# A planned gated-attention and mixture kernel: mixed inputs of the first block on TensorE, loads on a second queue, a wider search for the order

## The chip, the cores and the metric

The kernel runs on one core of one Trainium2 chip. The metric is device microseconds of one execution, and the median of three executions is given. A profile is of one execution more. Names in short: PE is TensorE (matrix products), DVE is VectorE, ACT is ScalarE, POOL is GpSimd, SP is the engine that issues transfers. PSUM is the memory that PE writes, in eight banks; SBUF is the memory on the chip that all engines read.

## What is computed

Three stages one after the other, each on the result of the one before: a gated linear attention over 8 heads of width 48, a mixture layer with a token shift, and a second mixture with a low-rank product over the tokens (4 batches, 768 tokens, 384 channels).

```python
for t in range(S):                                   # attention, for every head
    state = alpha[:, :, t, :, None] * state + einsum('bhd,bhe->bhde', k[:, :, t], v[:, :, t])
    y[:, :, t] = einsum('bhd,bhde->bhe', q[:, :, t], state)

x_prev = concatenate([zeros, x[:, :-1, :]], axis=1)  # first mixture
xk = mu_k * x + (1.0 - mu_k) * x_prev
xr = mu_r * x + (1.0 - mu_r) * x_prev
k = maximum(xk @ w_k, 0.0)
x = sigmoid(xr @ w_r) * (k * k @ w_v)

u = x + (x.transpose(0, 2, 1) @ U @ V).transpose(0, 2, 1)   # second mixture
out = u + maximum(u @ w_ch1, 0.0) @ w_ch2
```

The inputs are drawn so that alpha lies in 0.8 to 1.0. The attention of the fast path holds while alpha is at least 0.7072; the kernel checks this on its data and has a general path for the rest.

## The kernel before

**Tiling.** The 3072 tokens are 8 blocks of 384 (half a batch each). Attention works in units of two head pairs and 384 tokens (16 units, two to a block), a head pair being two heads in partitions 0 to 47 and 64 to 111 ("EV" and "OD"). A unit has two phases (`ph`), one for each head pair. For each phase `load_qka` brings q, k and alpha (one transfer for each head), `prep` makes decayed keys and queries with two scans on DVE (`L359`), `keys_by_token` transposes the keys on PE (`L320`), `scores` makes three 128x128 score tiles for each head on PE and masks them on DVE; for each unit `load_v` brings the values of the EV and of the OD heads in two transfers, `states` multiplies keys by values (`48x48`) and scans the sum, and `outputs` multiplies scores by values and states by queries and copies the result to x. Unit 1 stands before unit 0 in the first block (`first_attention`).

**Weights** come as 64-bit floats and are decoded on the chip in chunks of 128x384: two passes on ACT, two or three on DVE, of which the last (`split`) leaves a rounded high part and the rest as a low part. A product is three matrix products (`mm3`: high by high, high by low, low by high) in a rounded 32-bit type; nine of them of 384 columns make one tile of `moe1` or `moe2`.

**Mixed inputs** (`prep_mix`). In the first block each of the six tiles of xk and xr is `x_prev * (1 - mu)` on ACT, `x * mu + that` on DVE, and then a split on ACT and DVE.

**What sets the order.** Nothing is issued where it is written. Every operation is recorded with an engine, a cost in ns and a wished place (`plan.at`), and `Plan.issue` runs a list scheduler over the whole program: forward, then backward to get priorities, eleven times, and the order of the best forward pass is issued, so that each engine's queue is one fixed list. Where PE has nothing ready by the scheduler's costs, it puts in fillers, small bf16 products of a tile of zeros (`L405`), one for each 56 ns (112 ns in the first 4.5 us). These fillers are in PE's list for good: PE executes them whether or not there is anything to wait for.

**The end.** `check_range` reduces what the checks found, multiplies on PE (a 1x1 product) and casts the count on DVE into `ok_i` (`L1064`). `values_load` (`L407`) reads `ok_i` into a register of each engine, and `tc.If` (`L408`) branches past the general path. The mixed inputs' weights (`load_mu`) and all other transfers are issued from SP (`L376`).

```python
plan.act(t, x[:, kk, 0:TB], AF.Copy, scale=omm[:, j, kk : kk + 1])
plan.stt(t, x[:, kk, 1:], mu[:, j, kk : kk + 1], t, ALU.mult, ALU.add)
split(t, MIX[j][0][:, kk, :], MIX[j][1][:, kk, :], ...)
```

Of the kernel before, what the change touches and what calls it, by code (L numbers as in the profile page):

```python
# [8 lines left out]
F32 = mybir.dt.float32  # L9
# [10 lines left out]
P = 128  # L20
B, H, S, D = 4, 8, 768, 48
DM = 384
KD = 3
# [28 lines left out]
ROUNDS = 10  # L52
BATCH = 15000.0
# [27 lines left out]
class Plan:  # L81
# [7 lines left out]
    ENGINES = ("PE", "DVE", "ACT", "POOL", "SP")  # L89
    LAT = {"PE": 200.0, "DVE": 130.0, "ACT": 155.0, "POOL": 80.0, "SP": 1900.0}  # L90
    TO_PE = {"DVE": 250.0, "ACT": 270.0, "POOL": 200.0, "SP": 1900.0}
    OWN = {"PE": 0.0, "DVE": 127.0, "ACT": 150.0, "POOL": 100.0, "SP": 1900.0}
# [188 lines left out]
    def issue(self, filler=None, until=0.0, rounds=0):  # L281

        work = self.work
        n = len(work)
        after = [[] for _ in range(n)]
        before = [[] for _ in range(n)]
        for i, w in enumerate(work):
            for j in w[2]:  # L290
                lat = self.latency(j, i)
                after[j].append((i, lat))
                before[i].append((j, lat))
        n_after, n_before = [len(a) for a in after], [len(b) for b in before]
        prio = [w[4] for w in work]
        best = None
        for r in range(rounds + 1):
            order, times = self.schedule(after, n_before, prio, False, self.FILL, until)
            end = max(t for _, t in times)
            if best is None or end < best:  # L300
                best, self.order, self.times = end, order, times
            if r < rounds:
                _, back = self.schedule(before, n_after, [-t for _, t in times], True)
                prio = [-t if w[4] > self.AHEAD else w[4] for (_, t), w in zip(back, work)]
        for i in self.order:
            if i < 0:
                filler(-1 - i)
            else:
                self.run(*work[i][3])
# [12 lines left out]
    def act(self, out, in_, func, **kw):  # L322
# [3 lines left out]
        cost = (110.0 if in_.tensor.name in self.arenas else 68.0) + n * 0.833 + 95.0 * len(extra)  # L326
# [43 lines left out]
    def dma(self, out, in_, out_key=None, in_key=None, cost=650.0):  # L370
        words = 1
        for d in out.shape:
            words *= d
        self.add(
            "SP", max(cost, words / 56.0), [out if out_key is None else out_key], [in_ if in_key is None else in_key],
            lambda: self.nc.sync.dma_start(out, in_),  # L376
        )
# [3 lines left out]
def tile_gated_attention_moe(ctx, tc, qka, v, mus, w_k, w_r, w_v, U, V, w_1, w_2, out):  # L381
# [25 lines left out]
    n_ok = nc.values_load(ok_i[0:1, 0:1], min_val=0, max_val=2 * D, skip_runtime_bounds_check_because="a count of partitions")  # L407
# [4 lines left out]
def fast_path(nc, plan, arena, rounded, shared, banks, qka, v, mus, w_k, w_r, w_v, U, V, w_1, w_2, out, x2d, ok_i):  # L412
# [61 lines left out]
    Xs[1] = new(KD + 1, TB + 1)  # L474
    x2_ring = ring(2, DM)
# [187 lines left out]
    def load_mu():  # L663
        plan.dma(mu, mus, in_key="w")
        plan.dve(75, [omm], [mu], lambda: nc.vector.tensor_scalar(
            out=omm, in0=mu, scalar1=-1.0, scalar2=1.0, op0=ALU.mult, op1=ALU.add))

# [27 lines left out]
    def load_qka(ph, parts=((0, KD),), rows=D, to=None):  # L695
# [4 lines left out]
        for a, z in parts:  # L700
            for hh in range(2):
# [4 lines left out]
                    bass.AP(src.tensor, src.offset, [[KD * TB, n], [1, (z - a) * TB]]), in_key="in", cost=475.0,  # L706
# [134 lines left out]
    def first_attention():  # L841
# [3 lines left out]
        for i, u in enumerate((1, 0)):  # L845
# [5 lines left out]
            load_v(u)  # L851
            for j in range(2):
# [11 lines left out]
    def mm3(ps, lh, ll, rh, rl, first, last):  # L864
# [5 lines left out]
        plan.at = mm_at[0] - EARLY  # L870

# [196 lines left out]
    plan.at = -1640  # L1068
    load_mu()
# [21 lines left out]
    for n in range(NBLK):  # L1091
# [3 lines left out]
        if n:  # L1095
            prep_mix(n, (1, 0), start(n) - DUE["mix_r"], DUE["d1" if n == 1 else "d2" if n == 2 else "d"])
        else:
            prep_mix(n, (0,), start(n) - DUE["mix0_k"], "ACT")
            prep_mix(n, (1,), R0 - DUE["mix0_r"], "ACT")
# [309 lines left out]
```

## Time and profile before

| | |
|---|---|
| median of three executions | 699.4 us (698.97 to 699.49) |
| the profiled execution, its own time | 699.82 us |
| its span in the trace | 698.0 us |
| mean granted clock of PE | 0.998 of full speed |
| PE busy | 687.7 us (99%) |
| DVE, ACT, POOL busy | 479.9, 360.5, 66.8 us |
| moved by transfers | 55.14 MB |

The span reaches from the first to the last instruction that the profiler records; 1.8 us of the profiled execution's own time lie around it. PE's busy time counts the fillers too. A line such as `L138` or `L315` is that of a helper through which all operations of a kind go, so the rows are told apart by shapes and times. A matrix product of plain 32-bit floats is two records in the trace, one in the list of the order; a rounded one and a transpose are one record.

### The profile page before, as it was taken

The page shows a single profiled execution, that of the slowest core. Times are in us where ns is not written, and L with a number is a line of the kernel's source. Part 1 is how long each engine was busy: PE and PEld are TensorE (multiplying, and loading weights), DVE is VectorE, ACT ScalarE, POOL GpSimd, SP SyncE. Part 2 cuts the span into 40 slices and gives each one's busy share as a digit, 9 for nine tenths or more (in the row PEclk, how much of TensorE's full clock was granted, in tenths as well). Part 3 has the DMA queues.
Part 4 walks back from the last instruction along what each step waited for, and adds up shares of the span by engine and source line. Part 5 has one row for each costly group of instructions (what it writes and reads, how often), then busy time and mean ns, then how long its engine had stood idle before and what let it go on. Part 6 is the DMA issues. An engine that isn't in the chain of part 4 may idle for free.

```text
span 698.0 us, 13655 instructions
## 1 busy us (share of the span) xinstructions
PE 687.7 (99%) x5251; PEld 664.2 (95%) x5251; DVE 479.9 (69%) x1077; ACT 360.5 (52%) x895; POOL 66.8 (10%) x102
## 2 busy tenths in 40 slices
PE   9999999999999999999999999999999999999996
PEld 8899899999999999899999999999999999999996
DVE  7799898897567575663898976474858566574611
ACT  3779687868667586696997831111111212121210
POOL 2000104241211312101010100000000000000000
PEclk9999999999999999999999999999999999999999
DMA  8857674343231222313363502020100102020001
GB/s 193 209 140 193 145 168 132 93 133 76 78 80 50 85 70 77 78 40 99 96 193 91 147 1 69 0 69 2 58 12 11 58 1 69 0 69 1 36 1 38
DMA packets 29785, 55.14 MB, mean 79 GB/s; under 512 B 5360, under 2 KB 20816, under 8 KB 29712
## 3 DMA queue, kind: packets, MB, share of 16 engines
q1 hardware_dynamic: 29712, 54.19, 28.6%
q8 instruction: 43, 0.70, 0.4%
q14 instruction: 30, 0.25, 0.1%
HBM read 43.55 MB, written 9.44 MB: 76 GB/s over the span
## 4 chain that ended last, share of the span: by engine, by line
PE 85%; DVE 2%; ACT 1%; DMA 1%; issue 0%; SPq 0%; DVEq 0%; ACTq 0%
PE bank L315 84%; DMA arena<-in_qka_dram 1%; PE bank L320 1%; DVE shared L359 1%; ACT shared L330 1%; ACT arena L330 0%; DVE shared L138 0%; ACT bank L330 0%; DVE arena L138 0%; DVE rounded L138 0%; ACT rounded L330 0%; SPq L376 0%; DVE arena L730 0%; ACTq L330 0%; DVEq L138 0%
## 5 line engine op out<-in xcount | busy, mean ns | idle before, releaser
L315 PE MATMUL bank<-rounded 128*128 128x384 f32 x2232 | 421.1, 338 | 0.4 <-DVE rounded L138 0.4
L315 PEld LDWEIGHTS bank<-rounded 128*128 128x128 f32 x2232 | 383.1, 186 | 8.4 <-DVE rounded L138 1.2
L330 ACT ACTIVATE rounded<-bank 128x384 fp32r<-128x384 f32 x163 | 79.6, 489 | 188.8 <-PE bank L315 187.8
L315 PE MATMUL bank<-rounded,shared 128*128 128x384 f32 x864 | 164.5, 334 | 0.0
L315 PEld LDWEIGHTS bank<-rounded,shared 128*128 128x128 f32 x864 | 151.1, 188 | 0.0
L138 DVE SCALAR_TENSOR_TENSOR rounded<-bank,rounded 128x384 fp32r<-128x384 f32 x96 | 53.4, 556 | 105.1 <-ACT rounded L330 103.9
L330 ACT ACTIVATE arena<-arena 128x384 f32<-128x384 f32 (+5 forms) x234 | 102.2, 462 | 23.9 <-DMA arena<-in_qka_dram 16.7
L330 ACT ACTIVATE rounded<-arena 128x384 fp32r<-128x384 f32 (+3 forms) x134 | 68.6, 521 | 57.4 <-DVE arena L997 40.4
L997 DVE STREAM_TRANSPOSE arena<-arena 32x96 f32<-32x96 f32 x336 | 90.9, 271 | 5.0
L315 PEld LDWEIGHTS bank<-shared 128*48 128x48 f32 (+2 forms) x1408 | 75.7, 141 | 11.9 <-issue 6.9
L315 PE MATMUL bank<-shared 128*48 128x128 f32 (+3 forms) x1408 | 86.0, 264 | 0.2 <-DMA shared<-in_v_dram 0.2
L138 DVE SCALAR_TENSOR_TENSOR arena<-arena 128x384 int32<-128x384 int32 (+2 forms) x140 | 80.8, 592 | 7.9 <-ACT arena L330 7.2
L330 ACT ACTIVATE bank<-bank 128x384 f32<-128x384 f32 x128 | 61.0, 478 | 16.4 <-PE bank L315 15.1
L138 DVE TENSOR_TENSOR rounded<-bank,rounded 128x384 fp32r<-128x384 f32 x67 | 37.0, 552 | 39.5 <-ACT rounded L330 39.0
L359 DVE TENSOR_TENSOR_SCAN shared<-arena 112x384 f32<-112x384 f32 x64 | 60.8, 961 | 2.6 <-ACT arena L330 1.2
L138 DVE TENSOR_TENSOR rounded<-arena,rounded 128x384 fp32r<-128x384 f32 (+1 forms) x105 | 58.3, 564 | 4.4 <-ACT rounded L330 4.0
L138 DVE TENSOR_TENSOR arena<-bank,arena 128x384 f32<-128x384 f32 (+1 forms) x76 | 40.8, 550 | 20.2 <-PE bank L315 13.2
L330 ACT ACTIVATE arena<-bank 112x384 f32<-112x384 f32 (+3 forms) x62 | 28.7, 488 | 25.0 <-PE bank L315 24.5
L138 DVE TENSOR_TENSOR shared<-bank,arena 128x384 f32<-128x384 f32 x64 | 33.1, 547 | 9.4 <-PE bank L315 9.2
L138 POOL TENSOR_TENSOR rounded<-arena,rounded 128x384 fp32r<-128x384 f32 (+1 forms) x25 | 27.4, 1109 | 121.5 <-ACT rounded L330 107.4
L405 PE MATMUL bank<-warm 128*128 128x128 bf16 x584 | 37.4, 225 | 1.1 <-DVE arena L553 1.1
L405 PEld LDWEIGHTS <-warm 128*128 128x128 bf16 x584 | 35.2, 101 | 2.3 <-DVE arena L553 1.1
(48 smaller groups left out, 213.1 us busy)
## 6 DMA issues: line engine op xcount, KB each, us to landing
arena<-in_qka_dram SPq DMA_DIRECT2D x58, 216.0 KB, 3.9
arena<-in_w_dram SPq DMA_DIRECT2D x24, 384.0 KB, 3.5
shared<-in_v_dram SPq DMA_DIRECT2D x32, 144.0 KB, 2.4
x2d<-arena SPq DMA_DIRECT2D x24, 192.0 KB, 2.0
arena<-x2d SPq DMA_DIRECT2D x8, 576.0 KB, 4.1
out_dram<-arena SPq DMA_DIRECT2D x24, 192.0 KB, 1.9
arena<-in_w_v_dram SPq DMA_DIRECT2D x8, 384.0 KB, 3.8
arena<-in_w_k_dram SPq DMA_DIRECT2D x5, 384.0 KB, 7.6
```

The lines of the kernel that those rows point to most:

```text
L138: fn(**args)
L315: "PE", cost, [out], [lhsT, rhs], lambda out, lhsT, rhs: fn(out, lhsT=lhsT, rhs=rhs, start=start, stop=stop),
L320: self.add("PE", cost, [out], [in_, ident], lambda: self.nc.tensor.transpose(out, in_, ident))
L330: self.add("ACT", cost, outs, [in_] + extra, lambda out, in_: fn(out, in_, func, **kw), out=out, in_=in_)
L359: lambda: self.nc.vector.tensor_tensor_scan(out=out, data0=d0, data1=d1, initial=0.0, op0=op0, op1=op1), self.in_sbuf(d0, d1),
L405: lambda i: nc.tensor.matmul(banks[SPARE[i]][:, 384:512], lhsT=warm, rhs=warm, start=True, stop=True), FILL_UNTIL, ROUNDS
L997: plan.dve(284, [to], [src], lambda to=to, src=src: nc.vector.transpose(out=to, in_=src))
```

## The change

1. `n_ok = nc.values_load(...)` stands one level deeper, inside the scope of the tiles.
2. `Plan.issue` takes the best order of the eleven passes and makes 90 rounds more: the best order's priorities are shifted at random by up to 500 or 2000 ns, and three forward passes with two backward passes between them are tried. The best of all is issued.
3. A queue `ACTQ` is added: the OD loads of phases 2 and 3 (unit 1, the first to be needed) are issued from ACT. In the scheduler's costs ACTQ is a queue apart, that takes no time of ACT. A transfer's least cost is 580 ns where it was 650 (475 for q, k and alpha); a copy of a certain strided form on ACT costs more.
4. For the first block the mixed inputs are made on PE: `load_mu` is called early and makes 12 diagonal matrices (128x128) on ACT; `first_mix` multiplies each diagonal by x (two plain 32-bit products of 384 columns for each of six tiles, into banks 0, 1, 3 and 4), and the split reads the bank.

```diff
 ROUNDS = 10
+AROUND = 90
...
-        prio = [w[4] for w in work]
         best = None
-        for r in range(rounds + 1):
+
+        def there(prio):
+            nonlocal best
             order, times = self.schedule(after, n_before, prio, False, self.FILL, until)
             end = max(t for _, t in times)
-            if best is None or end < best:
-                best, self.order, self.times = end, order, times
...
+        prio = [w[4] for w in work]
+        for r in range(rounds + 1):
+            prio = back(there(prio))
+        rng = random.Random(1)
+        for r in range(AROUND):
+            far = (500.0, 2000.0)[r % 2]
+            prio = [p + rng.uniform(-far, far) if p > self.AHEAD else p for p in best[1]]
+            there(back(there(back(there(prio)))))
+        _, _, self.order, self.times = best
...
-        cost = (110.0 if in_.tensor.name in self.arenas else 68.0) + n * 0.833 + 95.0 * len(extra)
+        apart = in_.dtype == F32 and in_.ap[-1][0] == NC + 1
+        cost = (110.0 if in_.tensor.name in self.arenas else 68.0) + n * (2.2 if apart else 0.833) + 95.0 * len(extra)
...
-    n_ok = nc.values_load(ok_i[0:1, 0:1], min_val=0, max_val=2 * D, ...)
+        n_ok = nc.values_load(ok_i[0:1, 0:1], min_val=0, max_val=2 * D, ...)
...
         plan.dve(75, [omm], [mu], ...)
+        for j in range(2):
+            for kk in range(KD):
+                for a, t in enumerate((mu, omm)):
+                    plan.act(diag[:, a, j, kk], ident, AF.Copy, scale=t[:, j, kk : kk + 1])
...
-                    bass.AP(src.tensor, src.offset, [[KD * TB, n], [1, (z - a) * TB]]), in_key="in", cost=475.0,
+                    bass.AP(src.tensor, src.offset, [[KD * TB, n], [1, (z - a) * TB]]), in_key="in",
+                    queue="ACTQ" if hh and ph in (2, 3) and to is None else "SP",
...
+    def first_mix(j, due, into):
+        x = Xs[0]
+        for kk in range(KD):
+            plan.at = due + 3 * kk
+            ps = into[kk][:, 0:TB]
+            plan.mm(ps, diag[:, 0, j, kk], x[:, kk, 1:], True, False, 650.0)
+            plan.mm(ps, diag[:, 1, j, kk], x[:, kk, 0:TB], False, True, 650.0)
+            split(ps, MIX[j][0][:, kk, :], MIX[j][1][:, kk, :], "DVE")
...
-            prep_mix(n, (0,), start(n) - DUE["mix0_k"], "ACT")
-            prep_mix(n, (1,), R0 - DUE["mix0_r"], "ACT")
+            first_mix(0, start(n) - DUE["mix0_k"], (banks[0], banks[1], banks[3]))
+            first_mix(1, start(n) - DUE["mix0_k"] + 9, (banks[0], banks[1], banks[4]))
```

**Where the order moves.** On SP, after the first loads of phases 2 and 3, at the program's start, before the change (the names in brackets are the semaphores that a transfer waits for before it takes them itself; `in_v` rows are values, the first two those of unit 1):

```order
L376 DMA arena<-in_qka_dram 64x1152 [waits DMAHW0_49]
L376 DMA arena<-in_qka_dram 48x1152 [waits DMAHW1_49]
L376 DMA shared<-in_v_dram 128x288 [waits DMAHW2_49]
L376 DMA shared<-in_v_dram 128x288 [waits DMAHW3_49]
L376 DMA arena<-in_qka_dram 64x1152 [waits DMAHW4_49]
L376 DMA arena<-in_qka_dram 48x1152 [waits DMAHW5_49]
```

The same place after the change:

```order
L396 DMA shared<-in_v_dram 128x288 [waits DMAHW1_49]
L396 DMA arena<-in_qka_dram 48x1152 [waits DMAHW2_49]
L396 DMA arena<-in_qka_dram 64x1152 [waits DMAHW3_49]
L396 DMA arena<-in_qka_dram 48x1152 [waits DMAHW4_49]
L396 DMA arena<-in_qka_dram 64x1152 [waits DMAHW5_49]
L396 DMA shared<-in_v_dram 128x288 [waits DMAHW6_49]
```

And on PE after the change, the first products of keys by values (`48x48`, unit 1), with what they wait for (`bank_80<-shared 128x128` are the scores of phase 3's OD heads):

```order
L333 MATMUL bank_80<-shared 128x128 [waits DVE_49]
L333 MATMUL bank_80<-shared 128x128 x2
L425 LDWEIGHTS warm
L425 MATMUL bank_75<-warm 128x128
L333 MATMUL bank_78<-shared 48x48 [waits DMAHW6_49,Activation_49]
L333 MATMUL bank_78<-shared 48x48 [waits DMAHW1_49]
```

The two halves of unit 1's values stood together behind phase 0; now the four loads of phases 0 and 1 stand between them, and PE's first product waits for the later half. Ahead of that product PE's list holds 12 score products where it held 6, and 132 fillers where it held 126 (of both, 53 and 59 are the first run).

On PE, from the last outputs of the first attention on, after the change (`bank<-arena 128x384` are the products with a diagonal; `warm` are the fillers, of which one pair stands for each run of them):

```order
L333 MATMUL bank_80<-shared 48x128 x10
L333 MATMUL bank_76<-arena 128x384 x2
L333 MATMUL bank_77<-arena 128x384
L333 MATMUL bank_73<-arena 128x384 x2
L333 MATMUL bank_74<-arena 128x384 x2
L333 MATMUL bank_77<-arena 128x384
L333 MATMUL bank_76<-rounded 128x384
L425 LDWEIGHTS warm
L425 MATMUL bank_75<-warm 128x128
```

Before the change the fillers follow at once on the row `MATMUL bank_80<-shared 48x128 x10`. Counted over PE's whole list, there are 584 fillers before and 342 after. Up to the last product of the first attention they are 199 and 209 (the first run, in which PE starts, 59 and 53); from there to the first long run without fillers 385 and 108; and a run of 25 stands later, in the first block's products. The 12 products with a diagonal are the only real work added; 3168 products of 384 columns in the rounded type stand in both lists.

On DVE, at the program's end, before and after:

```order
L138 TENSOR_TENSOR arena<-bank_73,arena 128x384
L138 TENSOR_TENSOR arena<-bank_74,arena 128x384
L138 TENSOR_TENSOR arena<-bank_75,arena 128x384
L407 TENSOR_LOAD ok_i
L408 COMPARE_AND_BRANCH
```

```order
L140 TENSOR_TENSOR arena<-bank_73,arena 128x384
L140 TENSOR_TENSOR arena<-bank_75,arena 128x384
L140 TENSOR_TENSOR arena<-bank_74,arena 128x384
L1103 CAST ok_i<-bank_78 1x1
L427 TENSOR_LOAD ok_i
L428 COMPARE_AND_BRANCH
```

On ACT the list now begins with one of the four loads, the load of the function table (1.28 us in the trace before), a one-column activation and the other three loads, and only then come the two small copies that DVE's first scan waits for; the 12 diagonals stand among the copies that follow. DVE has 96 instructions ahead of its first square of block 0 before the change and 81 after it; ahead of the first of block 1 it has 202 and 195.

The register's load stands in the same place of every engine's list, behind the engine's last work; the cast that it waits for has moved to the end, behind the last sum (and the 1x1 product on PE behind the last product).

## Rows read from the trace of the kernel before

**Rows 1.** The page's first part: busy time, share, instructions of each engine.
```profile
PE 687.7 (99%) x5251; PEld 664.2 (95%) x5251; DVE 479.9 (69%) x1077; ACT 360.5 (52%) x895; POOL 66.8 (10%) x102
```

**Rows 2.** Windows: stretch, length, busy (instructions) of PE, PEld, DVE, ACT, POOL; clock, DMA share, GB/s.
```profile
4.30:20.00 15.70, 15.17 (x227) 13.81 (x224) 13.27 (x24) 5.53 (x19) 1.61 (x4) 1.00 1.00 252
...
33.00:45.00 12.00, 11.95 (x196) 11.32 (x193) 12.00 (x26) 11.20 (x28) 1.37 (x3) 1.00 0.47 102
```

**Rows 3.** The page's costliest groups: the fillers, busy us and mean ns.
```profile
L405 PE MATMUL bank<-warm 128*128 128x128 bf16 x584 | 37.4, 225 | 1.1 <-DVE arena L553 1.1
```

**Rows 4.** Timeline of PE, runs of fillers: start us, length us, what, count.
```profile
1.07 5.52 PE L405 MATMUL bank<-warm 128*128 128x128 bf16 x59 [1.07 <-DVE arena L553]
...
34.80 10.39 PE L405 MATMUL bank<-warm 128*128 128x128 bf16 x183
...
56.57 8.60 PE L315 MATMUL bank<-rounded 128*128 128x384 f32 x48
```

**Rows 5.** Timeline of PE: transposes, then scores of one phase (12 records, six products).
```profile
6.88 0.48 PE L320 MATMUL bank<-arena,shared 112*128 112x112 f32 x3 [0.29 <-DVE shared L138]
...
9.18 1.26 PE L315 MATMUL bank<-shared 48*128 48x128 f32 x12
```

**Rows 6.** The chain that ended last: the long run of rounded products, and its end.
```profile
364.02 327.62 PE bank L315 x1888
691.66 0.56 DVE arena L138
```

**Rows 7.** Timeline of the first 45 us: ACT's one run-up, SP's loads, DVE's first steps.
```profile
0.81 1.28 ACT L330 ACT_TABLE_LOAD   x1 [0.81 <-PEq L1394]
0.82 5.79 SPq L376 DMA_DIRECT2D arena<-in_qka_dram  x10
...
4.32 0.96 DVE L359 TENSOR_TENSOR_SCAN shared<-arena 112x384 f32<-112x384 f32 x1 [0.24 <-issue]
...
6.17 0.56 DVE L138 TENSOR_TENSOR shared<-arena,shared 112x384 f32<-112x384 f32 x1 [0.68 <-DMA arena<-in_qka_dram]
```

**Rows 8.** Timeline: unit 1's states, what they wait for, outputs, and unit 0's scan.
```profile
12.52 0.26 PE L315 MATMUL bank<-shared 128*48 128x48 f32 x2 [0.24 <-DMA shared<-in_v_dram]
...
14.45 0.96 DVE L359 TENSOR_TENSOR_SCAN shared<-bank,shared 112x384 f32<-112x384 f32 x1 [0.49 <-PE bank L315]
...
16.58 0.21 ACT L330 ACTIVATE arena<-arena 112x3 f32<-112x3 f32 x1 [0.58 <-DMA arena<-in_qka_dram]
...
16.79 2.58 PE L315 MATMUL bank<-shared 128*48 128x128 f32 x40
...
23.41 0.96 DVE L359 TENSOR_TENSOR_SCAN shared<-bank,shared 112x384 f32<-112x384 f32 x1 [0.39 <-PE bank L315]
```

**Rows 9.** Timeline: one mixed tile on ACT, on DVE, and DVE's first square.
```profile
30.83 0.61 ACT L330 ACTIVATE arena<-arena 128x384 f32<-128x384 f32 x1
...
31.48 0.62 DVE L138 SCALAR_TENSOR_TENSOR arena<-arena 128x384 f32<-128x384 f32 x1 [0.57 <-ACT arena L330]
...
54.98 0.56 DVE L138 TENSOR_TENSOR rounded<-bank,rounded 128x384 fp32r<-128x384 f32 x1
```

**Rows 10.** Who waited for whom, PE from 56 to 250 us: total, times, longest.
```profile
PE bank L320 <- ACT shared L330: 1.2, 1, 1.2
PE bank L320 <- DVE shared L359: 0.7, 1, 0.7
PE bank L315 <- DVE rounded L138: 0.4, 1, 0.4
```

**Rows 11.** Instructions of the count and of the branch: durations in ns, start in us.
```profile
L1064 DVE CAST ok_i<-bank x1: 136/136/136, 654.7 to 654.7; 1x1 int32<-1x1 f32 x1
...
L408 SPq EVENT_SEMAPHORE  x8: 17/17/17, 696.1 to 696.6; - x8
...
L408 PEldq COMPARE_BRANCH  x1: 3302/3302/3302, 689.0 to 689.0; - x1
```

**Rows 12.** Who waited for whom on SP, from 691 us to the end.
```profile
SPq L408 <- SPq L408: 2.9, 1, 2.9
```

More of the change, by code (lines that the diff above doesn't have):

```diff
@@ L1 @@
 import heapq
+import random
 from contextlib import ExitStack
@@ L81 @@
 class Plan:
[L89 to L92, printed above, removed]
+    ENGINES = ("PE", "DVE", "ACT", "POOL", "SP", "ACTQ")
+    LAT = {"PE": 200.0, "DVE": 130.0, "ACT": 155.0, "POOL": 80.0, "SP": 1900.0, "ACTQ": 1900.0}
+    TO_PE = {"DVE": 250.0, "ACT": 270.0, "POOL": 200.0, "SP": 1900.0, "ACTQ": 1900.0}
+    OWN = {"PE": 0.0, "DVE": 127.0, "ACT": 150.0, "POOL": 100.0, "SP": 1900.0, "ACTQ": 1900.0}
     FIRST = 700.0
@@ L294, in issue, with back @@
         n_after, n_before = [len(a) for a in after], [len(b) for b in before]
-        prio = [w[4] for w in work]
         best = None
-        for r in range(rounds + 1):
+        def there(prio):
+            nonlocal best
             order, times = self.schedule(after, n_before, prio, False, self.FILL, until)
             end = max(t for _, t in times)
-            if best is None or end < best:
-                best, self.order, self.times = end, order, times
-            if r < rounds:
-                _, back = self.schedule(before, n_after, [-t for _, t in times], True)
-                prio = [-t if w[4] > self.AHEAD else w[4] for (_, t), w in zip(back, work)]
+            better = best is None or end < best[0]
+            if better:
+                best = end, prio, order, times
+            return times
+        def back(times):
+            _, times = self.schedule(before, n_after, [-t for _, t in times], True)
+            return [-t if w[4] > self.AHEAD else w[4] for (_, t), w in zip(times, work)]
+        prio = [w[4] for w in work]
[7 more added lines that the diff above has]
+        _, _, self.order, self.times = best
         for i in self.order:
@@ L368, in pool, with dma @@
         self.add("POOL", cost, outs, ins, fn)
-    def dma(self, out, in_, out_key=None, in_key=None, cost=650.0):
+    def dma(self, out, in_, out_key=None, in_key=None, cost=580.0, queue="SP"):
         words = 1
@@ L374, in dma @@
         self.add(
-            "SP", max(cost, words / 56.0), [out if out_key is None else out_key], [in_ if in_key is None else in_key],
-            lambda: self.nc.sync.dma_start(out, in_),
+            queue, max(cost, words / 56.0), [out if out_key is None else out_key], [in_ if in_key is None else in_key],
+            lambda: (self.nc.sync if queue == "SP" else self.nc.scalar).dma_start(out, in_),
         )
@@ L406, in tile_gated_attention_moe @@
         )
-    n_ok = nc.values_load(ok_i[0:1, 0:1], min_val=0, max_val=2 * D, skip_runtime_bounds_check_because="a count of partitions")
+        n_ok = nc.values_load(ok_i[0:1, 0:1], min_val=0, max_val=2 * D, skip_runtime_bounds_check_because="a count of partitions")
     with tc.If(n_ok < 2 * D):
@@ L474, in fast_path @@
     Xs[1] = new(KD + 1, TB + 1)
+    diag = view(arena, top[arena.tensor.name], (2, 2, KD, P))
     x2_ring = ring(2, DM)
@@ L851, in first_attention @@
             load_v(u)
+            if i == 0:
+                plan.at = due - 799
+                load_mu()
             for j in range(2):
@@ L1067, in fast_path @@
     first_attention()
-    plan.at = -1640
-    load_mu()
     c0 = 0
```

## The prediction

> **What bounds the kernel now.** The page's first part comes first: PE is busy 99% of the span, DVE 69%, ACT 52% [rows 1]. So the time is PE's list, and the question is what in it is not needed. The groups give that: 584 fillers take 37.4 us [rows 3]. The timeline says where: the last run ends just before 56.57 us [rows 4], and from there PE runs on its products with hardly a wait (2.3 us in all up to 250 us [rows 10]) to the end of the chain, 1888 products in 327.62 us at the last stretch [rows 6]. The fillers stand in for waits: in the windows DVE is busy 12.00 of 12.00 us from 33 to 45, while PE runs fillers (its busy time says nothing there); and from 4.3 to 20 us the transfers are the limit, with a DMA share of 1.00 [rows 2]. So up to 56 us the bound is DMA first and DVE and ACT after it; behind that, PE. A gain can only come from the first 56 us, as fillers that are gone, and it counts in full at the end if nothing later takes their place. PE works at 2.4 GHz all through these windows (clock 1.00 [rows 2]); no term below uses another clock.
>
> **The change, part by part.** PE executes its list in order, so the sum is made on PE: what is gone from its list, what is added, and where it has to wait anew.
>
> Fillers. 242 are gone. Six are of the first run, 59 in 5.52 us, 0.094 each; 236 of the later kind, 183 in 10.39 us, 0.057 each [rows 4]. 6 x 0.094 + 236 x 0.057 = 14.0 us less. This is sure, since the list is fixed.
>
> Diagonal products. The trace has no plain 32-bit product of 128 rows by 384 columns. Its nearest row is a score: six products of 128 columns, two records each, in 1.26 us, 0.21 each [rows 5]; 384 columns are three times that, 0.63, and 12 of them 7.6 us. From below: at the pace of the rounded products, 327.62 / 1888 = 0.174 [rows 6], 2.1 us. From above: at the pace of the transposes, three of 112 columns in 0.48 [rows 5], 0.16 a record, so 0.55 for 384 columns and 1.10 for two records, 13.2 us. I take 7.6: the score is the same kind of product.
>
> What they replace. Six steps on ACT (0.61 [rows 9]) and six on DVE (0.62) are gone; the splits stay, reading a bank. These are 3.7 us of DVE's time just where it is full, and this is why the scheduler could drop fillers; it is not counted a second time. The 12 diagonals on ACT cost at most 12 x 0.61 = 7.3 us; ACT is idle 10.2 of the 15.7 us from 4.3 to 20 [rows 2], which hides them. Without that cover each delays the next copy of unit 1 by up to 0.6.
>
> Loads from ACT. ACT executes its list in order too. Ten issues at the start take 5.79 us on SP, 0.58 each [rows 7]; ACT's own price is not in the trace, and I take SP's. ACT then needs 0.81 + 0.58 + 1.28 (table) + 0.2 + 3 x 0.58 = 4.6 us until the two copies that DVE's first scan waits for. They took some 0.5, so the scan starts at 5.1 instead of 4.32 [rows 7]. The step behind it started at 6.17 after 0.68 us of waiting for a load, so most of the 0.8 is swallowed there: with the scan's 0.96 it can start at some 6.3. PE's first transposes move from 6.88 to 7.0 [rows 5], while PE, with six fillers less, would be there 0.6 earlier: those 0.6 come back as a wait, and 0.1 with them, +0.7. (From below 0, if an issue costs ACT nothing; the load of mu ahead of phase 3 lies in the same slack.)
>
> Values of unit 1. Their second half now stands behind the loads of phases 0 and 1. Before, the first product of keys by values started at 12.52, of which 0.24 was a wait for values [rows 8]. With 0.1 from above, 12 fillers more than before behind the first run (0.7) and six scores more (1.3), PE now gets there at 12.28 + 2.1 = 14.4. The transfers ahead of the second half are, with it, the same that stood up to phase 1's OD load before; the copy that waited for that load started at 16.58 after 0.58 of waiting [rows 8]. The DMA share of 1.00 says that bytes decide here and not issues [rows 2], so I put the landing at 16.5 and the wait at 2.1, 1.9 more than before. From below: if the four issues moved to ACT (2.3 us of SP's time) bring the transfers forward by as much, they land at 14.2 and the wait is 0.
>
> The Trainium skill has a rule for this (DMA: Bandwidth & Descriptors, Issuing engines are not separate DMA queues): transfers started from several engines run on the same 16 DMA engines and interleave, and only the issue time is saved. The trace agrees as far as it goes (share 1.00); by the rule the wait is the 1.9, by the scheduler's second queue it is the 0.
>
> Unit 1's outputs. Before, its scan started at 14.45 and the run of outputs that uses the states at 16.79 [rows 8], 2.3 later. With products from 16.5, the scan can't start before some 17.7 and those outputs before 20.0. PE meanwhile has the rest of the states, four outputs, 24 fillers and three transposes, some 2.8 to 3.5 us, and is there at 19.3 to 20: a wait of 0 to 0.7, I take 0.4.
>
> The search. It costs nothing on the chip. In blocks 1 to 7 PE's list has the same 3168 products and the same small ones in another order; the waits that it can remove are 2.3 us [rows 10], the largest behind the copy whose cost is now set higher. An order chosen as the best of some 280 by the scheduler's own costs has no margin against their errors, so it can as well make as many. Ends -2.3 and +2.3, I take 0.
>
> The register's load. It stands where it stood in every list, so it saves nothing: the change does not do here what its name says. What moves is the cast, 0.14 us [rows 11], which ran at 654.7 and now follows the last sum (691.66 + 0.56 [rows 6]). SP is still issuing then, and its path to the end is the longest: 2.9 us behind its branch [rows 12], and events until 696.6. PE's load and branch (3.3 us for the branch [rows 11]) used to lie under its last products; from 692.4 on the branch takes until 695.7, and 0.9 us are left for the load before PE would be later than SP. I take +0.1; if the five engines' branches, now all at once, hold SP up by as much as one of them took, +2.9.
>
> Sum: -14.0 + 7.6 + 0.7 + 1.9 + 0.4 + 0 + 0.1 = -3.3. Against the profiled execution's 699.82 that is 696.5; the median is 0.4 below that execution, so 696.1.
>
> A check from DVE's side: ahead of block 1's first square it has seven instructions less, at 0.56 [rows 9] 3.9 us. That bears the same size and no more.
>
> **The rivals.**
>
> The second queue works. The values land in time, neither they nor the outputs wait: -14.0 + 7.6 + 0.7 + 0.1 = -5.6, 693.8. For it: the first loads of a head leave at the same moment. Against it: the DMA share of 1.00.
>
> DVE takes it back. Unit 1's scan moves from 14.45 to some 17.7, and 11 of DVE's instructions lie between it and unit 0's scan: 0.96 + 2 x 0.96 + 9 x 0.56 = 7.9, so that comes at 25.6 instead of 23.41 [rows 8, 9]. Are these 2.2 not made up (two decode steps stand earlier, 1.1), PE waits at the first products of block 1 behind its 25 new fillers, and of DVE's 3.9 there remain 1.7: 697.7. For it: DVE full from 33 to 45. Against it: DVE idle 2.4 us of the window before 20 [rows 2], where work can move.
>
> A list without slack, slower. In blocks 1 to 7 each of 28 phases has transposes on PE that wait for DVE's product of keys. Where the new list puts them one DVE step (0.56 [rows 9]) too early, PE, which has no other list, waits that long; with 10 of 28 it costs 5.6, and -3.3 becomes +2.3: 701.7. From 3.3 / 28 = 0.12 us a phase it eats the gain. For it: waits of this kind stood before (1.2 and 0.7 at transposes [rows 10]). Against it: they were few among 28, under the same kind of list.
>
> Diagonal products at the transposes' pace (13.2 us) would give the same +2.3. For it: only that no row shows one. Against it: the scores.
>
> **How the numbers follow.** Forecast 0.56, second queue 0.2, DVE 0.12, list without slack 0.08, slow products 0.04. The likeliest case's own range is 694.6 to 697.6 (first waits 0 to 0.8, outputs 0 to 0.7, blocks 1 to 7 about 1 either way). The range for 8 in 10 goes down to the second queue's case with half a microsecond, 693.3, and up to the end of the DVE case, 698.9; the two slow cases stay out. About 0.2%, 1.4 us, is what a measurement can tell from no change: faster means under 698.0. Faster: forecast, second queue and half of the DVE case, 0.82; same is the other half with a little of the slow ones, 0.08; slower 0.10.
>
> **What would show it.** Fillers: 342, and PE's long run beginning some 3 to 5 us earlier than 56.57. Diagonal products: 24 records at some 0.32 us. Loads from ACT: DVE's first scan near 5.1, transposes near 7.0. Values: PE's first product of keys by values between 16 and 16.6 with a wait of about 2 us for `in_v`; if it starts near 14.4 without one, the second queue's case is right. Blocks 1 to 7: waits of PE of 1 to 4 us in all; 6 or more means the list has no slack. The end: from the last sum to the span's end 5.8 us as before, with the cast between. The prediction is wrong if the waits behind the fillers add up to more than 5 us, or the diagonal products to more than 9.

## The result, and the profile after

The changed kernel takes 709.42 us (median of 4 runs, 708.67 to 709.66) against 699.18 us for the kernel before in the same comparison: a ratio of 1.0146, 95% interval 1.0129 to 1.0164. It is 10.2 us slower where 3.1 us faster was forecast, and 10.5 us above the upper end of the range. The profiled execution took 708.67 us, 8.85 more than the one of before, and its span is 707.0 us.

The page's first part: busy us, share of the span and instructions of each engine.
```profile
PE 695.6 (98%) x5033; PEld 663.3 (94%) x5033; DVE 483.0 (68%) x1071; ACT 360.8 (51%) x901; POOL 66.6 (9%) x102
```
PE is still the bound [rows 1], with 218 records fewer (242 fillers less, 24 records of the diagonal products more) and 7.9 us more of busy time. The windows answer to [rows 2], with the same columns:
```profile
4.30:20.00 15.70, 14.11 (x212) 12.68 (x210) 13.24 (x27) 8.46 (x30) 1.01 (x4) 1.00 0.99 259
33.00:45.00 12.00, 12.00 (x102) 9.10 (x101) 11.29 (x24) 10.36 (x28) 0.49 (x3) 1.00 1.01 215
```
The head is what the prediction made of it: the transfers are at their limit until 20 us, ScalarE has 2.9 us more to do there and has room for it, VectorE is no longer full from 33 to 45 us, and PE runs at 2.4 GHz (clock 1.00 here, and 0.998 over the span in both profiled executions). One thing is new: from 33 to 45 us the transfers are at their limit as well (a share of 1.01, 0.47 before), but no wait of PE comes of it. So the loss is none of the clock's. It shows in the groups of PE's instructions, kept apart by shape: line, operation, names, shapes, count, then busy us and mean ns of one, then idle time before them.
```profile
L333 PE MATMUL bank<-shared 48*128 48x128 f32 x384 | 46.2, 290 | 0.0
L333 PE MATMUL bank<-shared 128*48 128x128 f32 x384 | 37.6, 276 | 0.0
L333 PE MATMUL bank<-shared 112*48 112x128 f32 x320 | 33.4, 273 | 0.0
L425 PE MATMUL bank<-warm 128*128 128x128 bf16 x342 | 24.0, 226 | 1.1 <-DVE arena L574 1.1
L338 PE MATMUL bank<-arena,shared 112*128 112x112 f32 x80 | 15.8, 264 | 1.6 <-DVE shared L140 1.6
L333 PE MATMUL bank<-arena 128*128 128x384 f32 x24 | 8.4, 492 | 0.0
```
The first row is the scores (384 records of 192 products), the second and third are the outputs. The same three groups of the kernel before:
```profile
L315 PE MATMUL bank<-shared 48*128 48x128 f32 x384 | 35.2, 289 | 0.0
L315 PE MATMUL bank<-shared 128*48 128x128 f32 x384 | 30.4, 275 | 0.0
L315 PE MATMUL bank<-shared 112*48 112x128 f32 x320 | 26.6, 272 | 0.0
```
The scores are as many and each record is as long; they cover 11 us more of the time because fewer of them run side by side. The fillers went from 37.4 [rows 3] to 24.0 us, near the forecast.

Busy times of groups overlap with each other (the outputs' two grow by 14.0 us, and PE loses 2.2 by them), so here is PE's time as a chain: for each kind of record, the time from its start to the start of PE's next record, summed over the trace (us; the columns on the right are experiments told below).

| kind | before | after | search off | search alone | in turn | three and three |
|---|---|---|---|---|---|---|
| fillers | 36.5 | 23.2 | 23.1 | 35.6 | 22.4 | 22.8 |
| scores | 32.8 | 43.0 | 34.4 | 42.5 | 27.8 | 38.2 |
| states | 9.4 | 10.2 | 9.5 | 11.2 | 9.7 | 9.4 |
| outputs | 40.4 | 42.6 | 40.7 | 41.9 | 41.0 | 41.0 |
| transposes | 7.0 | 6.1 | 6.8 | 5.5 | 5.4 | 5.4 |
| products of 384 columns | 563.2 | 573.0 | 569.7 | 563.8 | 573.1 | 570.6 |
| PE's last record starts at | 691.3 | 700.0 | 686.1 | 702.2 | 681.3 | 689.2 |

From before to after: fillers -13.4, scores +10.2, outputs +2.2, states +0.8, transposes -0.9, products of 384 columns +9.8 (7.4 of it the diagonals), together +8.7 on PE's last record; what follows it lasts 0.2 us longer. The diagonals take back more than half of what the fillers give, as forecast; the scores alone take the rest and more.

The time from one start to the next holds the waits in between too: 1.6 us of the fillers' 23.2 are waits behind them, 0.6 of the 36.5 before.

Why the scores? A score product has 48 rows: those of the first partition block (rows 0 to 47) or of the second (rows 64 to 111). In the kernel before, single records of a six whose products change block each time start in twos, 0.007 us apart, and the next two 0.112 later: six products in 0.87 us. Three of one block and then three of the other take 1.19. Three of one block with other work behind them take 0.86, with records 0.112 apart one by one, and a single product takes 0.41. Before, 19 of 32 phases ran at 0.87 to 0.97 for the six. After, of PE's 192 scores 63 stand in 21 sets of three of one block, and of the 19 sixes that are whole 14 take 1.19. Neighbours in PE's list that change block were 105 before and are 30 now. In the timeline of PE (start us, length us, what, count) here is a six of the kernel before, in turn, and then one of the kernel after, three and three:
```profile
321.49 0.94 PE L315 MATMUL bank<-shared 48*128 48x128 f32 x12
```
```profile
329.68 1.26 PE L333 MATMUL bank<-shared 48*128 48x128 f32 x12
```
The head after the change shows lone threes, where one six has become two threes with fillers between:
```profile
12.45 0.93 PE L333 MATMUL bank<-shared 48*128 48x128 f32 x6
13.32 1.18 PE L425 MATMUL bank<-warm 128*128 128x128 bf16 x18
14.43 0.93 PE L333 MATMUL bank<-shared 48*128 48x128 f32 x6
15.29 0.23 PE L425 MATMUL bank<-warm 128*128 128x128 bf16 x1
15.45 1.18 PE L333 MATMUL bank<-shared 128*48 128x48 f32 x32
```
The scheduler prices a score at 107 ns wherever it stands, so its search saw nothing lost when it drew the blocks apart.

The Trainium skill has the rule behind this (TensorE: Matmul & The Clock Gate, Part 3: Packing small matmuls — row/col tiling): products whose operands lie in different strips of 32 rows run at the same time, started some 4 ns apart, while products keep their program order. The trace agrees, with 0.007 us between the starts of two. The prediction had not weighed it.

### The profile page after: what moved, and what is told of

Read it like the earlier page. It is cut to its first block, busy times and chain, and to the rows that moved or that the text cites. A ratio compares the mean times of both kernels' runs of the same rounds, so it can differ in the third digit from the quotient of the medians.

```text
span 707.0 us, 13199 instructions
## 1 busy us (share of the span) xinstructions
PE 695.6 (98%) x5033; PEld 663.3 (94%) x5033; DVE 483.0 (68%) x1071; ACT 360.8 (51%) x901; POOL 66.6 (9%) x102
## 4 chain that ended last, share of the span: by engine, by line
PE 91%; DVE 3%; DMA 2%; ACT 2%; issue 1%; SPq 0%; ACTq 0%
PE bank L333 88%; PE bank L425 2%; DVE arena L140 1%; PE bank L338 1%; DVE rounded L140 1%; ACT rounded L349 1%; DMA arena<-in_w_dram 1%; DMA arena<-in_qka_dram 1%; DMA arena<-in_mu_dram 1%; DVE arena L1036 0%; ACT arena L349 0%; ACT bank L349 0%; DVE shared L140 0%; SPq L396 0%; DVE shared L378 0%
## 5 line engine op out<-in xcount | busy, mean ns | idle before, releaser
L333 PE MATMUL bank<-rounded 128*128 128x384 f32 (+1 forms) x2232 | 446.1, 339 | 1.7 <-DVE rounded L140 1.4
L333 PEld LDWEIGHTS bank<-rounded 128*128 128x128 f32 (+1 forms) x2232 | 385.2, 186 | 11.5 <-DVE rounded L140 2.0
L333 PE MATMUL bank<-rounded,shared 128*128 128x384 f32 x864 | 186.9, 334 | 0.2 <-DVE rounded L140 0.2
L349 ACT ACTIVATE arena<-arena 128x384 f32<-128x384 f32 (+6 forms) x240 | 102.9, 454 | 23.9 <-DMA arena<-in_qka_dram 9.5
L333 PE MATMUL bank<-shared 128*48 128x128 f32 (+3 forms) x1408 | 99.3, 265 | 0.0
L333 PEld LDWEIGHTS bank<-shared 128*48 128x48 f32 (+2 forms) x1408 | 85.1, 140 | 14.3 <-issue 8.0
L349 ACT ACTIVATE rounded<-arena 128x384 fp32r<-128x384 f32 (+2 forms) x128 | 65.3, 520 | 48.2 <-DVE arena L1036 31.2
L349 ACT ACTIVATE bank<-bank 128x384 f32<-128x384 f32 x128 | 61.3, 479 | 23.1 <-PE bank L333 22.0
L140 DVE TENSOR_TENSOR rounded<-arena,rounded 128x384 fp32r<-128x384 f32 (+1 forms) x99 | 54.0, 554 | 11.2 <-ACT rounded L349 9.5
L140 DVE TENSOR_TENSOR shared<-arena,shared 112x384 f32<-112x384 f32 (+1 forms) x57 | 33.7, 592 | 1.9 <-ACT shared L349 1.4
L349 ACT ACTIVATE shared<-shared 48x192 f32<-48x192 f32 (+2 forms) x40 | 23.3, 583 | 16.1 <-DVE shared L378 15.7
```

The costliest lines, as they stand in the source:

```text
L140: fn(**args)
L333: "PE", cost, [out], [lhsT, rhs], lambda out, lhsT, rhs: fn(out, lhsT=lhsT, rhs=rhs, start=start, stop=stop),
L349: self.add("ACT", cost, outs, [in_] + extra, lambda out, in_: fn(out, in_, func, **kw), out=out, in_=in_)
```

## The experiments

Theory A: the search lost the turn of the two blocks. Theory B: the loss lies in the new head (mu on the queue, ScalarE's loads, diagonals). "Before" is the median of the kernel before in the same comparison.

**The search off.**
```
-AROUND = 90
+AROUND = 0
```


> The changed kernel with the number of tries in the search set to 0, all else kept (early mu, second queue, diagonal products, new costs, load inside the planner's block). Theory A: the time was lost because the search scattered the score products; a score product of the first partition block (rows 0 to 47) and one of the second (rows 64 to 111) run at the same time on TensorE when they are issued in turn (six in 0.87 us), less so as three and three (1.19 us), and not at all when three of one block stand alone (0.86 us for three). Here about 18 of 32 sixes alternate again: the scores take some 34.5 us in place of 43.0, and the time is 699 to 702 us. Theory B: the time was lost in the head and in the diagonal products (24 records of 0.32 us, mu on the queue, copies by ScalarE): nothing of that is changed, so 707 to 710 us.

Measured 694.49 us (694.25 to 694.86; before 698.77; ratio 0.9945, interval 0.9928 to 0.9961). B falls. A's scores came as expected (34.4 us), but the time is 4.5 us below A's range: in the traces the search had also cost 1.8 us in the outputs, 0.7 in the states and 3.3 in the products of 384 columns (PE goes over from long to short products at 74 places with it and 66 without, and gaps of over 0.34 us behind a long product sum to 6.5 and 3.4 us). This plan has another order in the head too, so these sizes are those of two plans and not of single causes.

**The search alone**, put into the kernel before:
```
+AROUND = 90
...
+        for r in range(AROUND):
+            far = (500.0, 2000.0)[r % 2]
+            prio = [p + rng.uniform(-far, far) if p > self.AHEAD else p for p in best[1]]
+            there(back(there(back(there(prio)))))
```


> The kernel before with the search of 90 tries alone added (no early mu, no second queue, no diagonal products, old costs, register load after the fillers). Its order has 38 places where neighbouring scores change partition block, 105 in the kernel before and 30 in the changed one. Theory A: slower than before by 6 to 10 us, 705 to 709 us, with the scores at 40 to 43 us of TensorE's time. Theory B: the search reorders small work that fits anyway; 29 fewer fillers of 0.06 us: 697 to 699 us.

Measured 712.08 us (711.08 to 712.97; ratio 1.02, interval 1.0183 to 1.0217). Slower as A says, by 13.3 us and so by more than its 6 to 10; B falls: scores +9.7, states +1.8 and outputs +1.5 in the table. Nothing of the rest of the change is in this kernel, so the search makes the loss by itself.

**Six in turn**, one item of the plan, in the changed kernel with its search:
```
-        for c in range(NC):
-            cs = slice(c * CH, (c + 1) * CH)
-            for h, r in enumerate((EV, OD)):
-                plan.mm(sc[h][:, c, :], kb[r, cs], qg[r, cs], True, True, plan.SCORE)
+        plan.mms(
+            [
+                (sc[h][:, c, :], kb[r, c * CH : (c + 1) * CH], qg[r, c * CH : (c + 1) * CH], True, True)
+                for c in range(NC) for h, r in enumerate((EV, OD))
+            ],
+            plan.SIX,
+        )
```


> The changed kernel, but the six score products of a phase are one item of the plan (cost six times that of one), issued first block, second block, first block and so on. The search is on. Theory A: 32 sixes of 0.87 us are 27.8 us in place of 43.0: 694 to 698 us. Theory B: 707 to 710 us.

**Three and three**, the same plan with the order inside the item changed:
```
-                for c in range(NC) for h, r in enumerate((EV, OD))
+                for h, r in enumerate((EV, OD)) for c in range(NC)
```


> As the kernel with the six score products issued in turn, with the same plan, instruction for instruction, but inside each item the three products of the first partition block come first and then the three of the second. Theory A: 32 x (1.19 - 0.87) = 10.2 us slower than the kernel in turn, 704 to 708 us. Theory B, and any in which the order of the two blocks doesn't matter: equal to it within 0.2%.

In turn 689.87 us (689.19 to 691.14; ratio 0.988, interval 0.9863 to 0.9896); three and three 698.28 us (697.8 to 698.66; ratio 0.9994, interval 0.9985 to 1.0004). The two kernels differ in nothing but the order inside the items, and in 8.4 us. The timeline of PE at one phase, first in turn, then three and three:
```profile
46.31 0.69 PE L334 MATMUL bank<-rounded 128*128 128x384 f32 x3
46.92 0.94 PE L343 MATMUL bank<-shared 48*128 48x128 f32 x12
47.79 0.62 PE L334 MATMUL bank<-rounded 128*128 128x384 f32 x2
```
```profile
47.62 0.69 PE L334 MATMUL bank<-rounded 128*128 128x384 f32 x3
48.24 1.26 PE L343 MATMUL bank<-shared 48*128 48x128 f32 x12
49.43 0.61 PE L334 MATMUL bank<-rounded 128*128 128x384 f32 x2
```
From the scores' start to the next product it is 0.87 and 1.19 us, and so 32 times; the group rows of the two kernels, in the same order, say it in one line each, with an equal mean and a different busy time:
```profile
L343 PE MATMUL bank<-shared 48*128 48x128 f32 x384 | 30.0, 289 | 0.0
```
```profile
L343 PE MATMUL bank<-shared 48*128 48x128 f32 x384 | 40.4, 289 | 0.3 <-DVE shared L141 0.3
```
Of the 10.4 us between the scores, 2.5 come back in the products of 384 columns, which wait less when PE gets to them later. Both expected times were too high, by 4 us and more, since A had counted the scores alone (43.0 - 27.8 = 15.2 us): the plan with the item in it also lost 3.6 us less than the changed kernel's in outputs, states, transposes and fillers. So the 19.6 us between the changed kernel and the one in turn are not the turn alone; the 8.4 are.

**The lock alone**: the same item, in turn, in the kernel before.

> The kernel before, with nothing of the change, but the six score products of a phase as one item of the plan, issued in turn of the two partition blocks. Theory A: its scores take 32 x 0.87 = 27.8 us in place of 32.8, of which, as between the two kernels that differ in the turn alone (10.4 us of scores, 8.4 of time), some four fifths reach the end: 694 to 696 us. Rival: the new plan loses as much elsewhere, and the time stays at 698 to 699 us.

Measured 693.57 us (692.92 to 694.05; before 698.73; ratio 0.9925, interval 0.9906 to 0.9944): 5.2 us, of which the scores are 4.6 (32.8 to 28.2). That is just under A's range, and the rival falls. The kernel before had lost the turn in part, too.

**No diagonals**: six in turn and the search, with the old mix.
```
-            first_mix(0, start(n) - DUE["mix0_k"], (banks[0], banks[1], banks[3]))
-            first_mix(1, start(n) - DUE["mix0_k"] + 9, (banks[0], banks[1], banks[4]))
+            prep_mix(n, (0,), start(n) - DUE["mix0_k"], "ACT")
+            prep_mix(n, (1,), R0 - DUE["mix0_r"], "ACT")
```


> The kernel with six scores in turn and the search (689.9 us), but the first block's inputs are mixed by ScalarE and VectorE as in the kernel before, with mu still early and the second queue kept. It has 526 fillers in place of 346. Theory A (the forecast's own terms for the diagonals): 180 more fillers x 0.065 = +11.7 us, 24 records fewer x 0.323 = -7.8 us, together +4: 693 to 695 us. Rival: the mix on two engines is early enough with mu early, and only the products go: 682 to 684 us.

Measured 693.26 us (692.02 to 693.76; ratio 0.992, interval 0.9898 to 0.9942), 3.4 us above the kernel with diagonals. Fillers +10.5, products of 384 columns -7.7: the forecast's two terms, apart from the scores. The rival falls.

**In turn, search off.**
```
-AROUND = 90
+AROUND = 0
```


> The kernel with six scores in turn (689.9 us), with the number of tries in the search set to 0. Theory A: once the turn can't be broken, the search gains what its own count says or nothing: 22 more fillers of 0.065 us are +1.4, and the rest within 1.5 us: 689.5 to 693 us. Rival: the search also costs in the products of states and outputs (both grew in the changed kernel, by 0.8 and 2.2 us): without it 686 to 688 us.

Measured 689.01 us (688.03 to 689.85; ratio 0.9856, interval 0.9836 to 0.9876). That is under A's range and over the rival's. The interval overlaps that of the kernel with the search, so once the turn is locked the search neither gains nor loses by these runs. With the scores in turn on both sides, the change without its search is worth 693.57 - 689.01 = 4.6 us. Who waited for whom on PE (engine, what, line and releaser; us in total, times, longest us):
```profile
PE bank L334 <- DMA shared<-in_v_dram: 1.4, 1, 1.4
PE bank L436 <- DVE arena L585: 1.1, 1, 1.1
PE bank L349 <- DVE shared L141: 0.8, 1, 0.8
```
Here the wait for unit 1's values stands that the prediction had put into the changed kernel.

**All in turn**: the pairs of states and of outputs as items as well.
```
-                            plan.mm(y, vs[:, h, c, j, :], SC[ph % 4][:, h, c, :], True, alone, plan.S128)
+                            two.append((y, vs[:, h, c, j, :], SC[ph % 4][:, h, c, :], True, alone))
...
+                    plan.mms(two, plan.PAIR128)
```


> The kernel with six scores in turn (689.9 us), and also the two products (one of each partition block) of every state and of every output as one item each. Theory A: an output product that has its partner takes 0.109 us, 352 of them 38.4 us in place of 41.0, the states 9.3 in place of 9.7, and 11 fewer fillers are 0.7: 685.5 to 688 us. Rival: larger items leave waits of the same size, 689 to 691 us.

Measured 691.29 us (691.07 to 692.09; ratio 0.9893, interval 0.9875 to 0.991). A is wrong, and the time is at the upper end of the rival's: outputs 40.9 in place of 41.0 us. Two records of them take some 0.11 us in both kernels, whether they start 0.007 or some 0.04 us apart, so there was no turn left to win.

**The true price**, in turn and search off, then **with the search**:
```
-    SIX = 6 * SCORE
+    SIX = 870.0
```


> The kernel with six scores in turn and no search (689.0 us), with the planner told what a six costs in the trace: 870 ns in place of 6 x 107 = 642. Theory A: the plan keeps later work in step, 43 fewer fillers of 0.065 us are -2.8, and the rest within 1.5: 685 to 688 us. Rival: nothing in the plan hangs on that price, and the fillers that go leave the wait itself: 688.5 to 690 us.

> As the kernel with six scores in turn and the price of 870 ns, with the search of 90 tries on. Theory A: what is left against the search is that it cuts the long products into more pieces (83 places where a short product follows a long one against 65 without it, at 0.09 to 0.1 us each): 1 to 3 us slower than without it, 687 to 690 us. Rival: with the turn locked and priced the search gains: 683 to 686 us.

Search off 690.06 us (689.41 to 691.55; ratio 0.9868, interval 0.9852 to 0.9883): no gain, though 43 fillers are gone, and A is wrong; the products of 384 columns grew by 4.6 us. Search on 692.17 us (691.59 to 692.65; ratio 0.9901, interval 0.9885 to 0.9918), 2.1 us slower, a difference of the size that A gave, from a higher base, and only just apart by the intervals. The two profiled executions are only 0.4 us apart (691.55 and 691.95), so the traces can't place all of it: the outputs take 43.3 us in place of 41.3, which is the one kind that differs by over half a microsecond to the disadvantage of the search. The reason A gave, more pieces of long products, is not borne out (those products take 572.8 and 573.1 us).

**One queue**, in turn and search off:
```
-                    queue="ACTQ" if hh and ph in (2, 3) and to is None else "SP",
+                    queue="SP",
```


> The kernel with six scores in turn and no search (689.0 us), with the four first transfers of the second partition block on SyncE's queue again. Theory A: they stand between the others there at 0.6 us each, the first transposes come 1 to 2 us later, and what is behind them too: 689.5 to 691.5 us. Rival: the head hides it behind the transfers' own time and ScalarE is rid of 4 x 0.42 us: 687.5 to 689 us.

Measured 690.41 us (689.7 to 691.98; ratio 0.9879, interval 0.9859 to 0.9898), 1.4 us above the kernel with two queues, with intervals that overlap: a gain of the second queue is not shown. A's time came, its reason only in small part: the first transposes start at 6.77 us against 6.44.

**Values first**, made from the kernel with the true price and the search off:
```
-            plan.at = due - 790
+            plan.at = due - 799
             load_v(u)
             if i == 0:
-                plan.at = due - 799
                 load_mu()
```


> The kernel with six scores in turn, the price of 870 ns and no search, with the first unit's values asked for ahead of mu. The kernel without that price waited 1.4 us for in_v. Theory A: that wait, where it is left, goes, mu is some 1 us later and the diagonals still early enough: 0.5 to 1.5 us faster than the kernel it is made from, 684 to 687 us. Rival: mu's product on VectorE, which stands ahead of the first reciprocal, now holds the first transposes by about 1 us more, and the time is the same or 1 us more.

Measured 688.99 us (688.61 to 689.11; before 699.09; ratio 0.9853, interval 0.984 to 0.9867). It is 1.1 us below the kernel that it is made from, with overlapping intervals, and over A's range; the reason given does not hold: that kernel had no wait for `in_v` left. It and the plain kernel in turn without search (689.01) are the fastest versions, 10 us under the kernel before and 20 under the changed one.

## Why the prediction was wrong

The step that failed is "The search. It costs nothing on the chip", with its ends of -2.3 and +2.3. It counted the same products in another order and asked only whether PE would wait. Taken out of the change it gives back 14.9 us (709.42 - 694.49, two comparisons against the same kernel before); put into the kernel before it costs 13.3. In the changed kernel its largest part is the scores' lost turn (+10.2 us in the chain, 8.6 of it gone with the search); the rest, in outputs, states and long products, is measured, but what causes it is not shown. The order itself has a price on PE, and the row that the prediction took for a score, "0.21 each" [rows 5], was already that of a phase that ran as three and three.

The other steps, by the trace after. They come nearer, and in part by luck. The terms that are left when the waits for values and outputs are taken out of the sum, -14.0 + 7.6 + 0.7 + 0.1 = -5.6, measure -5.8 (fillers with the waits behind them, diagonals, end); the 2.3 us of those two waits are not there. Without the search the change is 4.3 us faster than before, and 4.6 with all scores in turn, but those kernels have other plans; that this lies near the sum of the other terms, -3.3, proves none of them.

*Fillers*, -14.0, and the wait ahead of the first transposes, +0.7: together measured -13.4, of which the waits are +1.0. *Diagonal products*, 7.6: 24 records at some 0.32 us, 7.4 in the chain. (The bound from below, 2.1, took one record a product; the two would give 4.2.)

*Loads from ACT*: right in the start of the transposes, wrong in the cause and in the wait. The timeline of the head (start us, length us, what, count, idle time before):
```profile
0.82 0.38 ACTq L396 DMA_DIRECT2D arena<-in_qka_dram  x1
...
1.07 4.40 PE L425 MATMUL bank<-warm 128*128 128x128 bf16 x53 [1.07 <-DVE arena L574]
...
1.23 1.28 ACT L349 ACT_TABLE_LOAD   x1 [1.23 <-PEq L1431]
1.30 0.86 ACTq L396 DMA_DIRECT2D arena<-in_qka_dram  x2
...
4.18 0.96 DVE L378 TENSOR_TENSOR_SCAN shared<-arena 112x384 f32<-112x384 f32 x1 [0.18 <-ACT arena L349]
...
5.35 2.48 SPq L396 DMA_DIRECT2D arena<-in_qka_dram  x4
6.22 0.17 DVE L686 TENSOR_SCALAR arena<-arena 128x6 f32<-128x6 f32 x1 [0.96 <-DMA arena<-in_mu_dram]
...
7.06 0.48 PE L338 MATMUL bank<-arena,shared 112*128 112x112 f32 x3 [1.59 <-DVE shared L140]
```
An issue takes 0.37 to 0.46 us of ScalarE's queue and not the 0.58 that was forecast, and the first scan starts at 4.18, not 5.1. But one minus mu stands ahead of the reciprocal in VectorE's list and waits 0.96 us for its load, which the prediction had put into the slack. So the transposes start at 7.06 (forecast 7.0). PE waits 1.59 us where 0.29 [rows 5] plus 0.7 was forecast, since the 53 fillers of the first run take 4.40 us and not 53 x 0.094 = 5.0.

*Values and outputs*, 1.9 and 0.4: neither wait is there. The first product of keys by values starts at 15.45 with none, and unit 1's scan at 16.24, ahead of the 17.7 thought possible. The second half of the values, issued at 8.00, landed 7.0 us later, at 15.02: between the two ends of the prediction, 16.5 and 14.2. At the forecast 14.4 PE would have waited 0.6 us for it; it came a microsecond later, because two lone threes of 0.86 us each stand ahead of that product (1.3 us had been put down for six scores) and, behind the first run, 20 fillers more than before, not 12. (Ahead of that product the list before holds 118 fillers, and not the 126 given with the change; 126 stand ahead of the second.) So the second queue's case came true in the waits, but in part only by PE's lateness. In the kernel in turn without search such a wait appears (1.4 us); in the one with the search, whose values stand elsewhere among the loads, it does not.

*DVE takes it back*: in part at most. Unit 0's scan starts at 24.37 where that case had 25.6; behind its 25 late fillers PE waits 1.1 us for VectorE, at 63.30, where that case had 2.2.

*Blocks 1 to 7*: no wait took the gain. From 56 to 250 us the waits of PE are fewer than in [rows 10]:
```profile
PE bank L333 <- DVE rounded L140: 1.1, 1, 1.1
PE bank L333 <- ACT rounded L349: 0.4, 1, 0.4
```
So the rival "a list without slack" had the right part of the change and of the program, and the wrong mechanism: waits, where it was the pace of the products. The sign "PE's long run beginning some 3 to 5 us earlier" says little: the first long run begins at 48.65 us, 7.9 earlier, but 25 fillers follow at 60.23, and the last of them starts at 61.58, 5.0 later than the last one before.

*The register's load*, +0.1: +0.2 behind PE's last record. The chain's end and SyncE's wait, answering to [rows 6] and [rows 12]:
```profile
413.51 286.55 PE bank L333 x1647
700.08 0.56 DVE arena L140
```
```profile
SPq L428 <- SPq L428: 3.4, 1, 3.4
```
The prediction had that the load saves nothing. SyncE's wait grew by 0.5 us, far from the 2.9 of the upper end. TensorE's branch took longer than in [rows 11], where the five did not stand together:
```profile
L428 PEldq COMPARE_BRANCH  x1: 4402/4402/4402, 701.4 to 701.4; - x1
```

## What to carry to other kernels

Where small products of different partition blocks alternate, the order is part of the speed: issue the partners as one item, so that no scheduler or search can part them. (That alone gave 5.2 us; giving the item its true price on top gained nothing here.) A search over orders is only as good as its costs; what these don't price, it will spend. When a change reorders the bound engine's list, compare for each shape the busy time and the mean of one record: an equal mean with more busy time is a sign of lost overlap that no view of waits shows. How much was lost is read from the times between starts, since busy times of interleaved groups count the same time twice.

## What the runs showed of the hardware that was not expected

- A product of 48 rows and 128 columns in plain 32-bit floats costs 0.145 us in a six in turn with those of the other partition block, 0.199 in a six as three and three, 0.287 in a lone three and 0.41 alone, each counted to the start of what follows. Over 192 of them, turn against three and three is 10.4 us of PE's time and 8.4 us of the kernel's.
- The issue of a load of q, k and alpha took 0.37 to 0.46 us on ScalarE's queue in the head, and 0.47 to 0.59 on SyncE's in the head of the kernel before. It is not a price of the engine alone: over the whole changed kernel SyncE's issues of such loads have a median of 0.41.
- A product of 128 rows by 384 columns in plain 32-bit floats is two records of 0.323 us each, against one of 0.174 in the rounded type.
